# One copy of 1024 columns instead of two of 512, for the last two scores of an attention phase

## The chip, the cores and the metric

The kernel runs on one core of a Trainium2 chip. The core has five engines with queues of their own: TensorE (PE, its loads of weights shown apart as PEld), VectorE (DVE), ScalarE (ACT), GpSimd (POOL) and SyncE (SP, which issues transfers here). Matmuls write to PSUM, which has 8 banks of 512 f32 columns on 128 partitions; ACT and DVE read them from there into SBUF. The metric is the device time of one execution in microseconds. A profile comes from one such execution.

## The reference

Two branches work on the same x (2048 rows of 512) and are mixed row by row:

```python
g = sigmoid((x * gate_w).sum(-1, keepdims=True))
a = softmax_attention(x, wqkv, H=32, Dh=16) @ wo
b = mixer_mlp(x, w1, b1, w2, b2)     # LayerNorm, then an MLP with gelu across the 2048 rows
out = g * a + (1 - g) * b
```

For each of 32 heads the attention takes the scores of all 2048 queries against all 2048 keys (inner size 16), their exp, the product with v, and a division by the row sums. This part holds the change.

## The kernel before, in words

The kernel first makes v, the keys, half of the queries and the first layer of the MLP, up to about 280 us. The attention then runs in `NG * PHASES` = 32 x 4 = 128 phases. A group (`grp`) is a pair of heads and one half of the 1024 + 1024 queries; each of its four phases (`ph`) takes 16 scores. A score is one matmul of 128 keys by 512 queries (f32 results, one bank), line 1067, and each score stands in one half of TensorE's rows. In the other half a dense matmul (line 1076, tile `dn`) runs beside it: the second layer of the MLP, late queries and the output projection are cut into lists of 14 or 12 of these.

The 16 scores of a phase have numbers, and the number says what becomes of them:

- `SINGLE` (0, 2, 4, 6, 7, 8): ACT takes the exp of one bank, line 1093, tile `p`.
- `EVAC` (1, 3, 5, 9, 14, 15): DVE copies the bank into the SBUF tile `pe`, line 1089; when all six are there, ACT takes the exp of the 3072 columns in place, line 1102.
- `TWO` (10, 11) and (12, 13): two neighbouring banks, tile `t`, one exp of 1024 columns by ACT, line 1031.

Then 64 matmuls of `apply_v` (line 963, tile `av`) multiply exps by v: first those held over from the phase before (the `pe` tile), then this phase's single exps and pairs. DVE adds `av` to the group's sum (line 985). The next phase's scores follow at once. So the `pe` tile is used a phase later than it is made.

Seven banks serve the scores (`BANKS = 7`), the eighth the dense matmuls. `shares(n)` gives the order in which a phase takes them. Scores 0 to 6 take `share[0]` to `share[6]`; 7, 8 and 9 take the first three again; 10 and 11 take `share[3]` and `share[4]`, 12 and 13 `share[5]` and `share[6]`; 14 takes `share[0]` and 15 `share[2]`, both under the name `u`; `av` takes `share[1]`, and this bank becomes `share[6]` of the next phase. A matmul that writes a bank waits until the last reader of the bank is done: score 14 for ACT's exp of score 7, score 15 for DVE's copy of score 9, `av` for ACT's exp of score 8. Each `t` pair waits for a copy of DVE and an exp of ACT.

The order of the work on each engine in the attention is that of the code (`manual_schedule`). `later`, `amid` and `calls` put other work between: `amid` stands ahead of the copies of scores 14 and 15 on DVE, `later` behind the exp of the 3072 columns. Where the list of dense matmuls has 12, the last scores come in the order 12, 13, 15, 14.

Of the kernel before, what the change touches and what calls it, by code (L numbers as in the profile page):

```python
# [9 lines left out]
F32 = mybir.dt.float32  # L10
# [13 lines left out]
P = 128  # L24
# [8 lines left out]
NB = 512  # L33
# [27 lines left out]
def gated_mix(ctx: ExitStack, tc: tile.TileContext, a_x, a_wqkv, a_wo, b_w1, b_b1, b_w2, b_b2, gate_w, out):  # L61
    nc = tc.nc
# [115 lines left out]
    with tc.tile_pool(name="vp", bufs=1, side="right") as pool:  # L178
# [143 lines left out]
        y, t, w = (pool.tile([P, NS], F32, name=n) for n in "ytw")  # L322
# [103 lines left out]
    with tc.tile_pool(name="gl", bufs=2, side="right") as gl:  # L426
# [74 lines left out]
        for f0, cs in order.items():  # L501
            n = min(NB, F - f0) // P
# [43 lines left out]
    for i, p in reversed(list(enumerate(ps))):  # L546
        u = out_pool.tile([P, D], F32, name="row", bufs=3)
# [329 lines left out]
    for t in range(NS):  # L877
        at = put(second_layer(t), at, [14] * 3)
        if queries:
            b, n = queries.pop(0)  # L880
# [39 lines left out]
    TWO = (10, 11), (12, 13)  # L920
# [3 lines left out]
    def shares(n):  # L924

        for one in range(0, BANKS, 2):
            lows = [k for k in range(one)][::2] + [k for k in range(one + 1, BANKS)][::2]
            for third in lows:
                if n in (third, third + 1):
                    first, second = (low for low in lows if low != third)  # L930
                    return [first, first + 1, one, second, second + 1, 2 * third + 1 - n, n]


    def regions():
        return tc.tile_pool(name="ps_s", bufs=1, space=PSUM, reuse_waits="tile")
# [54 lines left out]
    with tc.manual_schedule(engines=engines):  # L990
# [3 lines left out]
        for p in range(LAST + 1):  # L994
            grp, ph = divmod(p, PHASES)
            second = ph % 2
# [20 lines left out]
            in_turn = list(range(n_b)) + ([14, 15] if n_b == NSC - 2 else [12, 13, 15, 14])  # L1017
            qbs = {}
            for a, b in TURNS + HELD:
                if head[a] == head[b]:  # L1020
                    qbs[a], qbs[b] = 0, 1
                else:
                    zero, one = (a, b) if head[a] == 0 else (b, a)
# [3 lines left out]
            def exps(n):  # L1027
                pt = ptp.tile([P, 2, NB], F32, name="p2", bufs=len(TWO))
                where = [share[(j - BANKS) % BANKS] for j in (n - 1, n)]
                low = min(where)  # L1030
                pairs_done.append(nc.scalar.activation(pt, twos[low, low + 1], AF.Exp, scale=SCALE))  # L1031
                for j, k in zip((n - 1, n), where):
                    units[j] = *units[j][:3], pt[:, k - low, :]

            pairs_done = []
            evac = evp.tile([P, len(EVAC), NB], F32, name="pe")
            units = {}
            share = shares(spare)
            pool = regions()
            psum = pool.__enter__()  # L1040
            ones = [psum.tile([P, NB], F32, name=f"s{n}") for n in range(BANKS)]
            for n in in_turn:
                i, qb = head[n], qbs[n]
                c = at[i][qb]
                at[i][qb] += 1
                if n < TWO[0][0]:
                    if n >= BANKS:
                        ones[share[n - BANKS]] = psum.tile([P, NB], F32, name=f"s{share[n - BANKS]}")
                    s = ones[share[n % BANKS]]
                else:  # L1050
                    if n == TWO[0][0]:
                        pool.__exit__(None, None, None)
                        pool = regions()
                        psum = pool.__enter__()
                        twos = {}
                        for low in range(BANKS):
                            if low == share[1]:
                                av = psum.tile([P, NB], F32, name="av")
                            elif low in (share[0], share[2]):
                                twos[low] = psum.tile([P, NB], F32, name=f"u{low}")  # L1060
                            elif low not in twos:
                                two = psum.tile([P, 2, NB], F32, name=f"t{low}")
                                twos[low], twos[low + 1] = two[:, 0, :], two[:, 1, :]
                                twos[low, low + 1] = two
                    s = twos[share[2 if n == NSC - 1 else (n - BANKS) % BANKS]]
                rows_i = slice(i * HALF, i * HALF + ROWS)
                nc.tensor.matmul(  # L1067
                    s,
                    kt[grp][rows_i, c * P : (c + 1) * P],
                    qt[grp][rows_i, qb * NB : (qb + 1) * NB],  # L1070
                    start=True,
                    stop=True,
                )
                if n < n_b:
                    ps, a, b, begin, last, done = beside[n]
                    mm = nc.tensor.matmul(ps, a[half], b[half], start=begin and not second, stop=last and bool(second))  # L1076
                    if n == 0 and fence is not None:
                        tc.add_manual_dep(mm.ins, fence.ins.name, SYNC, reason=REASON)
                    if n == n_b - 1:
                        fence = nc.gpsimd.memset(token, 0.0)  # L1080
                        tc.add_manual_dep(fence.ins, mm.ins.name, SYNC, reason=REASON)
                if n == in_turn[-2]:
                    if n_b and second and beside[-1][-1] in between:
                        between[beside[-1][-1]]()
                    for what, *args in amid.get(p, ()):
                        what(*args)
                if n in EVAC:
                    pt = evac[:, EVAC.index(n), :]
                    nc.vector.tensor_copy(pt, s)  # L1089
                    units[n] = i, c, qb, pt  # L1090
                elif n in SINGLE:
                    pt = ptp.tile([P, NB], F32, name="p1", bufs=len(SINGLE))
                    one = nc.scalar.activation(pt, s, AF.Exp, scale=SCALE)  # L1093
                    if n == SINGLE[-1] and p:
                        tc.add_manual_dep(one.ins, earlier.ins.name, SYNC, reason=EARLY)
                    units[n] = i, c, qb, pt
                else:
                    units[n] = i, c, qb, None
                    if n in (TWO[0][1], TWO[1][1]):
                        exps(n)  # L1100
# [129 lines left out]
    with tc.If(far_off != 0):  # L1230
        with (
# [6 lines left out]
            for b in range(ND):  # L1238
                with tc.For_i(0, P // DH, 1) as hi:
# [11 lines left out]
                    for t in range(NS):  # L1251
                        s = ps_s.tile([P, S], F32, name="s")
# [11 lines left out]
                        for n in range(NQ):  # L1264
# [4 lines left out]
                            pt = pool.tile([P, NB // P, P], F32, name="pt")  # L1269
# [41 lines left out]
```

## Time and profile before

| | us |
|---|---|
| median of 3 runs | 1265.4 (1265.24 to 1265.51) |
| the profiled execution | 1265.31 |
| its span, first to last instruction | 1263.5 |
| TensorE's granted clock, mean | 0.999 |
| 128 phases, first to last score | from 277.5 to 1224.6 |

Each row of a timeline has start and length in us, engine, line, operation, result and operands, a count where neighbours are merged, and in brackets the idle time ahead of it and what ended it. Where several instructions stand in one row the length runs from the first start to the last end, and instructions of an engine may overlap. PE's ends are modelled; its loads of weights (PEld) show when a matmul was let go.

### The profile page before, as it was taken

The page shows a single profiled execution, that of the slowest core. Times are in us where ns is not written, and L with a number is a line of the kernel's source. Part 1 is how long each engine was busy: PE and PEld are TensorE (multiplying, and loading weights), DVE is VectorE, ACT ScalarE, POOL GpSimd, SP SyncE. Part 2 cuts the span into 40 slices and gives each one's busy share as a digit, 9 for nine tenths or more (in the row PEclk, how much of TensorE's full clock was granted, in tenths as well). Part 3 has the DMA queues.
Part 4 walks back from the last instruction along what each step waited for, and adds up shares of the span by engine and source line. Part 5 has one row for each costly group of instructions (what it writes and reads, how often), then busy time and mean ns, then how long its engine had stood idle before and what let it go on. Part 6 is the DMA issues. An engine that isn't in the chain of part 4 may idle for free.

```text
span 1263.5 us, 32833 instructions
## 1 busy us (share of the span) xinstructions
PE 1254.8 (99%) x13342; PEld 829.2 (66%) x13342; DVE 856.7 (68%) x1562; ACT 1069.0 (85%) x1405; POOL 198.6 (16%) x316
## 2 busy tenths in 40 slices
PE   9999999999999999999999999999999999999998
PEld 7888888875666666666666666666666666666656
DVE  5675453178767676767677677776777677678883
ACT  4443343269999999999999999999999999999990
POOL 0220444461010101010110101111111111000000
PEclk9999999999999999999999999999999999999999
DMA  4799443244744444544344433444543443366611
GB/s 134 251 340 329 143 122 106 81 127 110 214 121 104 90 102 85 158 86 97 77 105 94 99 90 83 91 87 81 113 101 73 90 100 60 56 166 175 151 60 70
DMA packets 100556, 152.32 MB, mean 121 GB/s; under 512 B 17109, under 2 KB 56171, under 8 KB 96300
## 3 DMA queue, kind: packets, MB, share of 16 engines
q1 hardware_dynamic: 99820, 149.08, 46.0%
q8 instruction: 107, 1.75, 0.6%
q10 hardware_dynamic: 576, 1.05, 0.2%
q14 instruction: 53, 0.43, 0.1%
HBM read 105.39 MB, written 44.68 MB: 119 GB/s over the span
## 4 chain that ended last, share of the span: by engine, by line
PE 96%; DVE 2%; ACT 1%; issue 0%; DVEq 0%
PE av L963 31%; PE s L1067 21%; PE acc L424 12%; PE t L1067 9%; PE acc L75 8%; PE t L963 5%; PE dn L1076 3%; PE u L1067 3%; PE pa L1162 2%; DVE pe L1089 1%; PE acc L199 1%; PE acc L268 0%; DVE ot L985 0%; PE acc L245 0%; ACT p L1093 0%; ACT pe L1102 0%
## 5 line engine op out<-in xcount | busy, mean ns | idle before, releaser
L1093 ACT ACTIVATE p<-s 128x512 f32<-128x512 f32 x768 | 411.9, 789 | 0.1
L1102 ACT ACTIVATE pe<-pe 128x3072 f32<-128x3072 f32 x129 | 380.9, 2954 | 0.0
L1067 PE MATMUL s<-qs,ks 64*128 64x512 f32 x1280 | 329.8, 400 | 0.6 <-ACT p L1093 0.6
L1089 DVE COPY pe<-s 128x512 f32<-128x512 f32 x512 | 323.6, 685 | 5.5 <-PE s L1067 1.5
L1067 PEld LDWEIGHTS s<-qs,ks 64*128 64x128 f32 x1280 | 225.7, 184 | 92.7 <-issue 52.3
L1031 ACT ACTIVATE p<-t 128x1024 f32<-128x1024 f32 x256 | 278.7, 1267 | 0.0
L963 PE MATMUL av<-p,v 128*32 128x256 f32 x3880 | 227.2, 379 | 0.0
L1089 DVE COPY pe<-u 128x512 f32<-128x512 f32 x256 | 164.8, 685 | 67.1 <-PE u L1067 67.1
L963 PE MATMUL av<-pe,v 128*32 128x256 f32 x3072 | 192.5, 383 | 0.0
L985 DVE TENSOR_TENSOR ot<-av,ot 128x512 f32<-128x512 f32 (+2 forms) x160 | 93.0, 582 | 140.9 <-PE av L963 139.6
L68 POOL TENSOR_TENSOR w_lo<-w_raw,w_hi 128x512 fp32r<-128x512 f32 (+1 forms) x128 | 153.0, 1202 | 196.8 <-ACT w_hi L67 99.9
L1076 PE MATMUL dn<-u_lo,w_hi 64*128 64x512 f32 x448 | 181.0, 404 | 0.0
L1076 PE MATMUL dn<-u_hi,w_hi 64*128 64x512 f32 x448 | 180.7, 403 | 0.0
L963 PEld LDWEIGHTS av<-p,v 128*32 128x32 f32 x3880 | 126.0, 110 | 83.3 <-ACT p L1093 0.2
L1076 PE MATMUL dn<-u_hi,w_lo 64*128 64x512 f32 x448 | 180.6, 403 | 0.0
L1067 PE MATMUL t<-qs,ks 64*128 64x512 f32 x512 | 142.5, 413 | 0.0
L963 PEld LDWEIGHTS av<-pe,v 128*32 128x32 f32 x3072 | 86.8, 109 | 80.7 <-ACT p L1093 35.7
L1080 POOL MEMSET token<- 1x1 f32 x128 | 11.3, 88 | 742.7 <-PE dn L1076 679.4
L67 ACT CAST w_hi<-w_raw 128x512 fp32r<-128x512 f32 (+1 forms) x67 | 38.0, 569 | 82.7 <-PE acc L424 63.1
L1067 PEld LDWEIGHTS t<-qs,ks 64*128 64x128 f32 x512 | 73.2, 184 | 50.8 <-ACT p L1093 48.6
L424 PE MATMUL acc<-h_hi,w_hi 128*128 128x512 f32 x224 | 87.9, 392 | 0.0
L424 PE MATMUL acc<-h_hi,w_lo 128*128 128x512 f32 x224 | 87.9, 392 | 0.0
(171 smaller groups left out, 1615.8 us busy)
## 6 DMA issues: line engine op xcount, KB each, us to landing
w_raw<-in_B_w_dram SPq DMA_DIRECT2D x96, 256.0 KB
ks<-kp SPq DMA_DIRECT2D x192, 128.0 KB
qs<-qp SPq DMA_DIRECT2D x256, 64.0 KB
kp<-pc SPq DMA_DIRECT2D x16, 512.0 KB
qp<-pc SPq DMA_DIRECT2D x8, 768.0 KB
qp<-row SPq DMA_DIRECT2D x24, 256.0 KB
v<-v SPq DMA_DIRECT2D x4, 1088.0 KB
x<-in_A_x_dram SPq DMA_DIRECT2D x16, 256.0 KB
```

What stands on the lines that cost most here:

```text
L67: copy(hi, src)
L68: return sub(lo, src, hi.bitcast(F32), ALU.subtract)
L75: nc.tensor.matmul(ps, a, b, start=start and n == 0, stop=stop and n == last)
L424: nc.tensor.matmul(p, a, b, start=first and k == 0, stop=last and k == 2)
L963: mm = nc.tensor.matmul(av[32 * j : 32 * (j + 1), i * QC : (i + 1) * QC], vb[b][:, v_at : v_at + 32], pt[:, h * QC : (h + 1) * QC], start= ...
L985: latest["add"] = nc.vector.tensor_tensor(x, y, x, ALU.add)
L1031: pairs_done.append(nc.scalar.activation(pt, twos[low, low + 1], AF.Exp, scale=SCALE))
L1067: nc.tensor.matmul(s, kt[grp][rows_i, c * P : (c + 1) * P], qt[grp][rows_i, qb * NB : (qb + 1) * NB], start=True, stop=True,)
L1076: mm = nc.tensor.matmul(ps, a[half], b[half], start=begin and not second, stop=last and bool(second))
L1089: nc.vector.tensor_copy(pt, s)
L1093: one = nc.scalar.activation(pt, s, AF.Exp, scale=SCALE)
L1102: done = nc.scalar.activation(x, x, AF.Exp, scale=SCALE)
```

## The change

`shares` now puts the neighbour of the first bank third and the odd bank second, so that scores 14 and 15 stand in neighbouring banks and `av` in the odd one. The two banks become one tile of 1024 columns, still named `u`. The four copies of scores 1, 3, 5 and 9 stay as they are; scores 14 and 15 are copied by one operation, issued behind the later of the two, into the last two slots of `pe`, which are neighbours already.

```diff
-                    return [first, first + 1, one, second, second + 1, 2 * third + 1 - n, n]
+                    return [first, one, first + 1, second, second + 1, 2 * third + 1 - n, n]
...
                             if low == share[1]:
                                 av = psum.tile([P, NB], F32, name="av")
-                            elif low in (share[0], share[2]):
-                                twos[low] = psum.tile([P, NB], F32, name=f"u{low}")
                             elif low not in twos:
-                                two = psum.tile([P, 2, NB], F32, name=f"t{low}")
+                                two = psum.tile([P, 2, NB], F32, name=f"{'u' if low == share[0] else 't'}{low}")
                                 twos[low], twos[low + 1] = two[:, 0, :], two[:, 1, :]
                                 twos[low, low + 1] = two
...
                 if n in EVAC:
                     pt = evac[:, EVAC.index(n), :]
-                    nc.vector.tensor_copy(pt, s)
+                    if n < TWO[0][0]:
+                        nc.vector.tensor_copy(pt, s)
+                    elif n == in_turn[-1]:
+                        nc.vector.tensor_copy(evac[:, -2:, :], twos[share[0], share[2]])
                     units[n] = i, c, qb, pt
```

On TensorE the end of a phase's scores stood like this (names: `t` and `u` the tiles above, `dn` the dense matmul, `av` the product with v; in brackets the semaphores of the engines that the instruction waits for):

```order
L1067 MATMUL t_4040<-qs,ks 128x512 [waits DVE_49,Activation_49]
L1076 MATMUL dn<-u_hi,w_lo 128x512
L1067 MATMUL t_4040<-qs,ks 128x512
L1076 MATMUL dn<-u_hi,w_hi 128x512
L1067 MATMUL u_4038<-qs,ks 128x512 [waits Activation_49]
L1067 MATMUL u_4037<-qs,ks 128x512 [waits DVE_49]
L963 MATMUL av<-pe,v_111 32x256 [waits Activation_49]
```

The same place now:

```order
L1065 MATMUL t_4016<-qs,ks 128x512 [waits DVE_49,Activation_49]
L1074 MATMUL dn<-u_hi,w_lo 128x512
L1065 MATMUL t_4016<-qs,ks 128x512
L1074 MATMUL dn<-u_hi,w_hi 128x512
L1065 MATMUL u_4017<-qs,ks 128x512 [waits DVE_49,Activation_49]
L1065 MATMUL u_4017<-qs,ks 128x512
L963 MATMUL av<-pe,v_111 32x256 [waits Activation_49]
```

The order is the same; the two waits, which stood on one u score each, now stand together on the first. On DVE a phase had, from the sum's addition to the small instruction behind the copies (`mark`):

```order
L985 TENSOR_TENSOR ot<-av,ot 128x512 [waits PE_49]
L1089 COPY pe<-s_3131 128x512 [waits PE_49]
L1089 COPY pe<-s_3132 128x512 [waits PE_49]
L1089 COPY pe<-s_3128 128x512 [waits PE_49]
L1089 COPY pe<-s_3169 128x512 [waits PE_49]
L1089 COPY pe<-u_3179 128x512 [waits PE_49]
L1089 COPY pe<-u_3177 128x512 [waits PE_49]
L1111 MEMSET mark 1x1 [waits DVE_49,Activation_49,Pool_49]
```

And now:

```order
L985 TENSOR_TENSOR ot<-av,ot 128x512 [waits PE_49]
L1088 COPY pe<-s_3121 128x512 [waits PE_49]
L1088 COPY pe<-s_3124 128x512 [waits PE_49]
L1088 COPY pe<-s_3120 128x512 [waits PE_49]
L1088 COPY pe<-s_3161 128x512 [waits PE_49]
L1090 COPY pe<-u_3171 128x1024 [waits PE_49]
L1112 MEMSET mark 1x1 [waits DVE_49,Activation_49,Pool_49]
```

The last two copies are one row; nothing else moved on DVE.

## The prediction

> **What bounds the kernel now.** I read the page first, then a table by stage, then the timeline of single phases on each engine. All rows are of the kernel before.
>
> ```profile
> span 1263.5 us, 32833 instructions
> PE 1254.8 (99%) x13342; PEld 829.2 (66%) x13342; DVE 856.7 (68%) x1562; ACT 1069.0 (85%) x1405; POOL 198.6 (16%) x316
> L1102 ACT ACTIVATE pe<-pe 128x3072 f32<-128x3072 f32 x129 | 380.9, 2954 | 0.0
> L1089 DVE COPY pe<-u 128x512 f32<-128x512 f32 x256 | 164.8, 685 | 67.1 <-PE u L1067 67.1
> ...
> 308.20:1109.40 801.20, 801.12 (x10124) 493.43 (x10120) 572.15 (x1072) 801.20 (x973) 91.63 (x195) 1.00 0.45 100
> 1116.90:1221.20 104.30, 103.74 (x1292) 63.96 (x1288) 88.99 (x160) 104.26 (x127) 3.78 (x18) 1.00 0.59 147
> ```
>
> The last two rows are stretches of the attention phases: length, then busy time of PE, PEld, DVE, ACT and POOL, clock, DMA. PE and ACT are both busy to the last hundredth in the first, so the share of busy time cannot say which of them sets the pace. DVE, from which the change takes work, has 229 us free there (801.2 - 572.2): its time in itself is worth nothing.
>
> What sets the pace is read from one phase, here the one that starts at 805.26.
>
> ```profile
> start us, us, engine line op out<-in xcount [idle before <-releaser]
> 805.26 0.18 PEld L1067 LDWEIGHTS s<-qs,ks 64*128 64x128 f32 x1 [0.41 <-issue]
> 807.72 1.32 ACT L1093 ACTIVATE p<-s 128x512 f32<-128x512 f32 x2
> 807.86 0.69 DVE L1089 COPY pe<-s 128x512 f32<-128x512 f32 x1
> 808.20 0.84 ACT L1093 ACTIVATE p<-s 128x512 f32<-128x512 f32 x1
> 808.60 0.19 PEld L1067 LDWEIGHTS u<-qs,ks 64*128 64x128 f32 x2 [0.19 <-ACT p L1093]
> 809.09 0.16 PEld L963 LDWEIGHTS av<-pe,v 128*32 128x32 f32 x8 [0.30 <-ACT p L1093]
> 809.13 1.29 DVE L1089 COPY pe<-u 128x512 f32<-128x512 f32 x2 [0.58 <-PE u L1067]
> 810.51 3.01 ACT L1102 ACTIVATE pe<-pe 128x3072 f32<-128x3072 f32 x1
> 812.68 0.18 PEld L1067 LDWEIGHTS s<-qs,ks 64*128 64x128 f32 x1 [0.41 <-issue]
> ```
>
> The sixth and last single exp of ACT (score 8) runs from 808.20 to 809.04; its bank is the one that `av` takes, and the first weight load of `av` is at 809.09, 0.05 later. From there 64 `av` matmuls lead to the next phase's first load at 812.68. So ACT's exps hold `av`. The u scores are loaded at 808.60, 0.05 after DVE's fourth copy ended (807.86 + 0.69 = 808.55), and between u load and `av` load lie 0.49 us.
>
> Whether those 0.49 are needed is shown by the last phases, where ACT is not the limit:
>
> ```profile
> 1124.52 0.18 PEld L1067 LDWEIGHTS s<-qs,ks 64*128 64x128 f32 x1 [0.41 <-issue]
> 1126.49 0.68 DVE L1089 COPY pe<-s 128x512 f32<-128x512 f32 x1
> 1126.52 0.61 ACT L1093 ACTIVATE p<-s 128x512 f32<-128x512 f32 x1
> 1127.29 0.18 PEld L1067 LDWEIGHTS t<-qs,ks 64*128 64x128 f32 x1 [0.15 <-ACT p L1093]
> 1127.14 0.69 DVE L1089 COPY pe<-s 128x512 f32<-128x512 f32 x1
> 1127.88 0.19 PEld L1067 LDWEIGHTS u<-qs,ks 64*128 64x128 f32 x2 [0.38 <-DVE pe L1089]
> 1128.32 0.16 PEld L963 LDWEIGHTS av<-pe,v 128*32 128x32 f32 x8 [0.25 <-ACT p L1093]
> 1146.67 0.18 PEld L1067 LDWEIGHTS s<-qs,ks 64*128 64x128 f32 x1 [0.41 <-issue]
> 1154.32 0.18 PEld L1067 LDWEIGHTS s<-qs,ks 64*128 64x128 f32 x1 [0.41 <-issue]
> 1176.43 0.18 PEld L1067 LDWEIGHTS s<-qs,ks 64*128 64x128 f32 x1 [0.41 <-issue]
> ```
>
> Here `av` follows the u load by 1128.32 - 1127.88 = 0.44. So in the long stretch only 0.05 us of slack lies behind the u load. The rows name a second loop, of PE and DVE alone: first score, fourth copy of DVE, u load, `av`, next first score. Its length where nothing else holds it is that of the phases 1124.52 to 1146.67 and 1154.32 to 1176.43, three each: (22.15 + 22.11) / 6 = 7.377 us.
>
> ```profile
> 308.24 0.18 PEld L1067 LDWEIGHTS s<-qs,ks 64*128 64x128 f32 x1 [0.41 <-issue]
> 1116.87 0.18 PEld L1067 LDWEIGHTS s<-qs,ks 64*128 64x128 f32 x1 [0.41 <-issue]
> ```
>
> From 308.24 to 1116.87 there are 109 phases, (1116.87 - 308.24) / 109 = 7.419 each. So ACT's loop is 7.419, the loop of PE and DVE 7.377; the second is covered by 0.042 us a phase.
>
> **The change, part by part.**
>
> *The copy.* Two copies of 512 columns took 1.29 us together (809.13). One of 1024 is not in the trace; its price is bounded by these rows:
>
> ```profile
> L1119 DVE TENSOR_TENSOR e<-o_sum,e 128x1024 fp32r<-128x1024 f32 x2 | 2.4, 1218 | 0.0
> L1119 DVE CAST e<-o_sum 128x1024 fp32r<-128x1024 f32 x2 | 1.4, 691 | 0.0
> L985 DVE TENSOR_TENSOR ot<-av,ot 128x512 f32<-128x512 f32 x95 | 65.6, 690 | 134.4 <-PE av L963 134.1
> L985 DVE TENSOR_TENSOR ot<-av,ot 128x256 f32<-128x256 f32 x34 | 14.2, 421 | 5.5 <-PE av L963 5.5
> ```
>
> At least 0.69 (a cast within SBUF), at most twice 0.685 = 1.37. From PSUM, 256 more columns cost 690 - 421 = 269 ns, so 512 more on a copy of 685 give 685 + 538 = 1.22, as the operation of 1024 columns has; I take 1.22. It saves 0.07 a phase on an engine that isn't on either loop: 0. The fused copy starts only after both scores; PE issues these two together (u x2, one row), so that costs 0 too.
>
> *ACT's exp of 3072 columns* waits for the copies: it starts at 810.51, 0.09 after their end at 810.42. Its start does not set ACT's pace, as one late start shows:
>
> ```profile
> 861.50 1.30 ACT L1031 ACTIVATE p<-t 128x1024 f32<-128x1024 f32 x1
> 862.73 2.77 ACT L1102 ACTIVATE pe<-pe 128x3072 f32<-128x3072 f32 x1
> 864.61 0.18 PEld L1067 LDWEIGHTS s<-qs,ks 64*128 64x128 f32 x1 [0.41 <-issue]
> 872.07 0.18 PEld L1067 LDWEIGHTS s<-qs,ks 64*128 64x128 f32 x1 [0.41 <-issue]
> ```
>
> There it starts 0.07 before its forerunner's end (862.80); in the phase above it started 0.36 before (L1031's pair ran to 810.87). So it is 0.29 late, and the phase behind it lasts 7.46, only 0.04 more than 7.419. ACT holds some 0.25 us of work in hand there, and a start that moves by some hundredths costs or gains 0.
>
> *The banks.* Score 14, 15 and `av` change places among the banks. Every bank but that of `av` is released long before it is written: the last copy ended at 810.42, the next phase's first load is at 812.68. The bank of `av` stays last in the next phase's order, as before. 0.
>
> *The wait of the u scores.* This is the part that costs. Before, score 14 waits for ACT alone and score 15 for DVE alone. As one tile both waits stand on the first of them, as they stood on each `t` pair already. PE then spends an instruction on the second wait:
>
> ```profile
> L1067 PEldq EVENT_SEMAPHORE  x297: 51/51/51, 274.7 to 1223.9; - x149
> ```
>
> 297 of them before, 51 ns each, two a phase for the two `t` pairs; now a third. Its price where DVE is the later releaser is read from the phase at 1124.52: the `t` load with two waits comes at 1127.29, 0.12 after DVE's copy (1127.17; ACT was done at 1127.13), the u load with one wait comes at 1127.88, 0.05 after its copy (1127.83). So 0.07, between 0.05 (the 51 ns alone) and 0.08 (two roundings of 0.01 each way); I take 0.06, between the instruction's own length and the difference. A gain is excluded, since the wait is only added. Behind this wait PE's own queue stands: both u loads, `av`'s 64 matmuls, then the next scores.
>
> **The sum.** In the 109 phases of the long stretch the loop of PE and DVE grows from 7.377 to 7.437 and overtakes ACT's 7.419: 0.018 x 109 = 2.0 us. ACT then runs out of its work in hand and waits, which costs nothing more. In the phases after 1116.87, 15 with the last, DVE releases the u load already (the row at 1127.88 says so): 0.06 x 15 = 0.9. The first four phases wait for other things: 0. Together 2.9 us. The profiled execution took 1265.31 (its span of 1263.5 and 1.8 around it); the median of the three runs, 1265.4, stands 0.1 above. 1265.3 + 2.9 = 1268.2, or 0.23% more. With 0.05 as the price it is 109 x 0.008 + 15 x 0.05 = 1.6, so 1266.9; with 0.08, 109 x 0.038 + 15 x 0.08 = 5.3, so 1270.6.
>
> **The rivals.**
>
> *The wait is hidden.* If PE resolves the wait for DVE ahead, or it is ACT's that goes into the extra instruction, `av` moves by two hundredths at most where ACT is the limit, and not at all in the last phases: ACT's fifth exp (807.72, the first of the two, some 0.83 long) ends with DVE's copy at 808.55, so `av` would come at 808.55 + 0.12 + 0.44 = 809.11 against 809.09. In the long stretch that is between 0 and 109 x 0.02 = 2.2 us, 1265.3 to 1267.5. For it: the covered 0.05 is real. Against it: the `t` loads put DVE's wait in front, in the same order of names as the u load now has. The Trainium skill, VectorE: DVE Perf Modes, § The DRAIN you can't avoid, says of a row of DVE copies that "the semaphore costs nothing extra here". By that rule, carried over to PE, the time would stay at 1265.3; the trace has 0.12 against 0.05 for two waits and one on PE, so I don't carry it over.
>
> *Faster: ACT's long exp starts earlier.* Its place is the start at 810.51. If the u load weren't later, the fused copy would end at 809.13 + 1.22 = 810.35 in place of 810.42. The second exp of 1024 columns could let its follower in at 810.48 (the pair's start 808.67 plus twice 0.91, the spacing of the two: 2.20 - 1.29), so 0.03 earlier in 128 phases: 3.8 us, 1261.5. It decides from the point where ACT's pace hangs on that start. For it: ACT is never idle, and the exp does start 0.09 behind the copy. Against it: the 0.29 that cost 0.04, and the u scores' 0.06, which uses up the 0.07 saved.
>
> *Slower by more: the fused copy ends late.* At 1.37 and 0.06 later it would end at 810.56, 0.14 late; if half of it came through in the 109 phases, that is 7.6 on top of the 2.9, 1275.8. The Trainium skill, Perfetto Trace Analysis, § Optimizing Scalar/DVE Operations, says that where DVE isn't saturated but causes bubbles, breaking up instructions may let work end sooner; that speaks against fusing. The same 0.29 that cost 0.04 says that ACT doesn't feel 0.14.
>
> **How the numbers follow.** The forecast's mechanism has 0.60, the hidden wait 0.28, ACT's earlier exp 0.08, the late copy 0.04. About 0.2%, or 2.5 us, is what a measurement of this kernel can tell from no change; the bound above is 1267.9. The forecast's own bounds, 1266.9 to 1270.6, lie mostly above it: 0.52 of its 0.60 I put to slower and 0.08 to no change. Slower is then 0.52 + 0.04 = 0.56, same 0.28 + 0.08 = 0.36, faster 0.08. The range takes in the hidden wait and the upper bound of the forecast with 0.2 to 0.3 for the spread of runs: 1265.0 to 1270.8. It leaves out the third and fourth case.
>
> **What the profile after would show.** The waiting instructions of the scores' line rise from 297 by 128 to about 425. The u load stands 0.12, not 0.05, behind DVE's fourth copy, and its releaser is DVE in nearly all phases. The phases of the long stretch last 7.43 to 7.44, those of the end 0.06 more each. The fused copy takes 1.22 and ends at the same place in the phase as the two did; ACT's exps show shorter records, since they no longer queue. The forecast is wrong if the phases stay at 7.419 (the wait is hidden), if the u load moves and `av` does not follow it by 0.44, or if the exp of 3072 columns comes to hold the next phase's first score.

## The result, and the profile after

The changed kernel takes 1271.31 us in the median of 5 runs (1271.18 to 1272.25), against 1265.44 (1265.24 to 1265.51) for the kernel before on the same chip: 1.0046 times as long, with a 95% interval of 1.0033 to 1.0058. The prediction was 1268.2, in a range up to 1270.8. The profiled execution took 1271.31, with a span of 1269.5 (before 1263.5), at the same granted clock of 0.999. An execution now and then has a lower granted clock and is longer, as is one of those given below, 1280.94 us at 0.948.

The page of the kernel after: busy time of the engines, the chain that ended last, and three of its costliest groups.

```profile
PE 1256.6 (99%) x13342; PEld 844.4 (67%) x13342; DVE 849.0 (67%) x1434; ACT 1073.9 (85%) x1405; POOL 198.9 (16%) x316
PE 91%; DVE 7%; issue 1%; DMA 0%; ACT 0%; SPq 0%; DVEq 0%; ACTq 0%
L1094 ACT ACTIVATE p<-s 128x512 f32<-128x512 f32 x768 | 390.9, 622 | 0.0
L1103 ACT ACTIVATE pe<-pe 128x3072 f32<-128x3072 f32 x129 | 356.4, 2764 | 1.1 <-DVE pe L1090 0.9
L1090 DVE COPY pe<-u 128x1024 f32<-128x1024 f32 x128 | 156.7, 1225 | 79.7 <-PE u L1065 79.1
```

The fused copy takes 1.225 us, and DVE is less busy by 7.7 us (856.7 to 849.0). Yet the span is 6.0 us longer. ACT's records of 3072 columns fell from a mean of 2954 to 2764 ns, though the operation is the same: part of the longer record was waiting in ACT's own queue (rows of ACT that show it stand with the rivals below).

The first loads of the phases that begin and end the long stretch, and the stretches as the kernel after has them (columns as in the prediction):

```profile
308.36 0.18 PEld L1065 LDWEIGHTS s<-qs,ks 64*128 64x128 f32 x1 [0.41 <-issue]
1121.49 0.18 PEld L1065 LDWEIGHTS s<-qs,ks 64*128 64x128 f32 x1 [0.41 <-issue]
308.36:1121.49 813.13, 810.65 (x10216) 512.98 (x10212) 570.37 (x973) 812.93 (x982) 91.79 (x195) 1.00 0.45 100
1121.49:1227.01 105.52, 103.68 (x1293) 64.29 (x1289) 88.37 (x146) 104.87 (x127) 3.79 (x18) 1.00 0.56 143
```

The same 109 phases took 813.13 us instead of 808.63, or 7.460 each instead of 7.419: +4.5 us. The next 14 took 105.52. Before, by the trace's nanoseconds, these 14 took 104.37, so +1.14. The first four phases add 0.15, and the last phase and what follows it 0.23: 0.15 + 4.49 + 1.14 + 0.23 = 6.0. The share of busy time still says nothing of who sets the pace: ACT shows 812.93 of 813.13, though, as the next rows show, it is ahead of its work now.

The waiting instructions of the scores' line, in the list of that line's instructions (count, shortest, median and longest in ns):

```profile
L1065 PEldq EVENT_SEMAPHORE  x424: 51/51/51, 274.7 to 1230.3; - x142
```

There were 297, so 127 were added. And the end of one phase, the one that starts at 808.13:

```profile
808.13 0.18 PEld L1065 LDWEIGHTS s<-qs,ks 64*128 64x128 f32 x1 [0.41 <-DVE big L68]
808.66 3.05 ACT L1094 ACTIVATE p<-s 128x512 f32<-128x512 f32 x6
808.89 2.53 DVE L1088 COPY pe<-s 128x512 f32<-128x512 f32 x4
811.53 0.22 PEld L1065 LDWEIGHTS u<-qs,ks 64*128 64x128 f32 x2 [0.31 <-ACT p L1094]
811.99 1.02 PEld L963 LDWEIGHTS av<-pe,v 128*32 128x32 f32 x24 [0.24 <-ACT p L1094]
812.10 1.22 DVE L1090 COPY pe<-u 128x1024 f32<-128x1024 f32 x1 [0.68 <-PE u L1065]
813.41 2.77 ACT L1103 ACTIVATE pe<-pe 128x3072 f32<-128x3072 f32 x1
815.58 0.18 PEld L1065 LDWEIGHTS s<-qs,ks 64*128 64x128 f32 x1 [0.41 <-issue]
```

Three things are to be seen. ACT's six single exps end at 808.66 + 3.05 = 811.71, and `av` is loaded 0.28 later, at 811.99; before, it was 0.05 later. ACT no longer holds `av`. DVE's fourth copy ends at 808.89 + 2.53 = 811.42 and the u load comes at 811.53, 0.11 to 0.12 behind. (The bracket names ACT, whose exp of score 7 was done long before; the wait is for DVE.) And the row of the two u loads is 0.22 long, not 0.19: one load takes 0.183, so the second begins 0.033 behind the first, where it had been 0.003.

In the trace's nanoseconds a phase's loop, from first score to next first score, is made of these parts. "Late, before" is the mean of the six phases from which the prediction took 7.377:

| part of the loop, us | late, before | long stretch, after (mean of 109) |
|---|---|---|
| first score to the end of DVE's fourth copy | 3.297 | 3.295 |
| to the first u load | 0.053 | 0.116 |
| to the second u load | 0.003 | 0.033 |
| to the first `av` load | 0.430 | 0.423 |
| to the next phase's first score | 3.593 | 3.593 |
| sum | 7.376 | 7.460 |

The added wait costs 0.063 at the first load and 0.030 more at the second, less 0.007 at `av` and 0.002 at the copy, 0.084 in all.

### The profile page after: what moved, and what is told of

Same layout as the page of the kernel before. It is cut to its first block, busy times and chain, and to the rows that moved or that the text cites. A ratio compares the mean times of both kernels' runs of the same rounds, so it can differ in the third digit from the quotient of the medians.

```text
span 1269.5 us, 32832 instructions
## 1 busy us (share of the span) xinstructions
PE 1256.6 (99%) x13342; PEld 844.4 (67%) x13342; DVE 849.0 (67%) x1434; ACT 1073.9 (85%) x1405; POOL 198.9 (16%) x316
## 4 chain that ended last, share of the span: by engine, by line
PE 91%; DVE 7%; issue 1%; DMA 0%; ACT 0%; SPq 0%; DVEq 0%; ACTq 0%
PE av L963 30%; PE s L1065 18%; PE acc L424 12%; PE acc L75 8%; PE t L1065 7%; PE t L963 5%; DVE pe L1088 5%; PE u L1065 4%; PE dn L1074 3%; PE pa L1163 2%; DVE ot L985 1%; PE acc L199 1%; PE acc L268 0%; DMA x<-in_A_x_dram 0%; DVE e L1120 0%
## 5 line engine op out<-in xcount | busy, mean ns | idle before, releaser
L1094 ACT ACTIVATE p<-s 128x512 f32<-128x512 f32 x768 | 390.9, 622 | 0.0
L1103 ACT ACTIVATE pe<-pe 128x3072 f32<-128x3072 f32 x129 | 356.4, 2764 | 1.1 <-DVE pe L1090 0.9
L1031 ACT ACTIVATE p<-t 128x1024 f32<-128x1024 f32 x256 | 256.7, 1095 | 0.0
L1090 DVE COPY pe<-u 128x1024 f32<-128x1024 f32 x128 | 156.7, 1225 | 79.7 <-PE u L1065 79.1
L1065 PE MATMUL t<-qs,ks 64*128 64x512 f32 x512 | 135.3, 398 | 0.0
L1065 PEld LDWEIGHTS t<-qs,ks 64*128 64x128 f32 x512 | 81.4, 184 | 32.4 <-ACT p L1094 22.6
```

Source lines behind the costliest of these rows:

```text
L1065: nc.tensor.matmul(s, kt[grp][rows_i, c * P : (c + 1) * P], qt[grp][rows_i, qb * NB : (qb + 1) * NB], start=True, stop=True,)
L1090: nc.vector.tensor_copy(evac[:, -2:, :], twos[share[0], share[2]])
L1103: done = nc.scalar.activation(x, x, AF.Exp, scale=SCALE)
```

## The experiments

The theory is that the added waiting instruction on the first u score makes the whole loss. Its rivals are that the new banks, or the fused copy that can begin only when both scores are there, have a part in it. The first four kernels tell these apart; the last two ask why the price is 0.084 a phase and not 0.06.

**Banks alone.** The kernel before, with nothing but the new order of banks; scores 14 and 15 stay two tiles, with two copies.

```diff
-                    return [first, first + 1, one, second, second + 1, 2 * third + 1 - n, n]
+                    return [first, one, first + 1, second, second + 1, 2 * third + 1 - n, n]
```

> The kernel before with the new order of the banks alone: scores 14 and 15 in neighbouring banks, av in the odd one, but two tiles u with a wait each, and two copies. Theory (the two waits on one load cost the time): the time of before, 1265.4 within 0.5, and phases of 7.419 us in the long stretch. Rival, the banks: all of the loss, 1271.3. Rival, the fused copy: the time of before.

Measured: 1265.32 us (1264.92 to 1266.4, 11 runs), a ratio of 1.0 (0.9991 to 1.0009). The banks cost nothing. The list of the score line's instructions has the old count:

```profile
L1067 PEldq EVENT_SEMAPHORE  x297: 51/51/51, 274.4 to 1223.4; - x149
```

**One tile, two copies.** The kernel after, but with the two banks copied out by two operations of 512 columns, issued together behind the last score.

```diff
                     elif n == in_turn[-1]:
-                        nc.vector.tensor_copy(evac[:, -2:, :], twos[share[0], share[2]])
+                        for m, where in enumerate((share[0], share[2])):
+                            nc.vector.tensor_copy(evac[:, len(EVAC) - 2 + m, :], twos[where])
```

> The changed kernel with the one tile u, so with both waits on its first load, but copied out by two copies of 512 issued together. Theory: the time of the changed kernel, 1271.3 within 0.7, since the first u load still stands 0.116 us behind DVE's fourth copy and the second 0.033 behind the first. Rival, the fused copy delays ACT's exp of 3072 columns: back to 1265.4. Rival, the banks: 1271.3.

Measured: 1271.6 (1271.42 to 1271.98), ratio 1.0049 (1.0035 to 1.0062), phases of the long stretch 7.459. The loss stands without the fused copy. The phase that starts at 808.13 here too:

```profile
811.52 0.21 PEld L1065 LDWEIGHTS u<-qs,ks 64*128 64x128 f32 x2 [0.30 <-ACT p L1095]
812.10 1.29 DVE L1091 COPY pe<-u 128x512 f32<-128x512 f32 x2 [0.69 <-PE u L1065]
813.48 2.77 ACT L1104 ACTIVATE pe<-pe 128x3072 f32<-128x3072 f32 x1
815.58 0.18 PEld L1065 LDWEIGHTS s<-qs,ks 64*128 64x128 f32 x1 [0.41 <-issue]
```

The two copies take 1.29 where the one took 1.22, and ACT's long exp starts 0.07 later (813.48, not 813.41). The next phase starts at 815.58 in both: what the fused copy saves is worth 0 here.

**The wait alone.** The kernel before, with its banks, two tiles and two copies, and both waits set on the first issued u score.

```diff
+                if n == in_turn[-2]:
+                    for other in (7, 9):
+                        tc.add_manual_dep(score.ins, done_with[other].ins.name, SYNC, reason=EARLY)
```

(`done_with` holds the copy or exp that read each score.)

> The kernel before, old banks and two copies, with nothing but both waits put on the first u score that is issued (for ACT's exp of score 7 and DVE's copy of score 9); the second u score then waits for nothing of its own. Theory: the whole loss, 1271.3 within 0.7, phases of 7.45 to 7.46 us. Rivals, banks or fused copy: 1265.4.

Measured: 1271.14 (1271.02 to 1271.5), ratio 1.0045 (1.0031 to 1.0059). The long stretch has 7.460 a phase, as after. The list of the line's instructions, and the u and `av` loads of the phase that starts at 808.11:

```profile
L1067 PEldq EVENT_SEMAPHORE  x424: 51/51/51, 274.7 to 1230.3; - x142
...
811.52 0.21 PEld L1067 LDWEIGHTS u<-qs,ks 64*128 64x128 f32 x2 [0.31 <-ACT p L1097]
811.97 1.02 PEld L963 LDWEIGHTS av<-pe,v 128*32 128x32 f32 x24 [0.24 <-ACT p L1097]
```

The wait alone gives the whole loss. Of the changed kernel's three parts (banks, one copy, one wait), this is the one that counts.

**The wait moved.** The kernel after, with the wait for ACT's exp of score 7 set on score 13, ahead of the u scores; the first u score then has DVE's wait only.

```diff
+                if n == TWO[1][1]:
+                    tc.add_manual_dep(score.ins, done_with[7].ins.name, SYNC, reason=EARLY)
```

> The changed kernel with the wait for ACT's exp of score 7 put on score 13, two matmuls ahead, which waits for nothing else; the first u load then waits for DVE alone. Theory: the u load stands 0.053 us behind DVE's copy again and the second 0.003 behind it, and the time is that of before or up to 1.2 us above it (1265.4 to 1266.6), since score 13 now waits for ACT and ACT has less work in hand. Rivals, banks or fused copy: 1271.3.

Measured: 1266.28 (1265.96 to 1280.94, 11 runs), ratio 1.0018 (0.9997 to 1.004): not to be told from no change, and 5 us below the kernel after. The phases have 7.4205 on the mean. The list, and loads, copies and ACT's last single exp of the phase whose u load is at 1128.53:

```profile
L1065 PEldq EVENT_SEMAPHORE  x296: 51/51/51, 274.9 to 1224.9; - x148
...
1127.79 0.69 DVE L1090 COPY pe<-s 128x512 f32<-128x512 f32 x1
1128.09 0.65 ACT L1096 ACTIVATE p<-s 128x512 f32<-128x512 f32 x1
1128.30 0.18 PEld L1065 LDWEIGHTS t<-qs,ks 64*128 64x128 f32 x1 [0.18 <-ACT p L1096]
1128.53 0.19 PEld L1065 LDWEIGHTS u<-qs,ks 64*128 64x128 f32 x2
1128.96 1.02 PEld L963 LDWEIGHTS av<-pe,v 128*32 128x32 f32 x24 [0.25 <-ACT p L1096]
1129.08 1.22 DVE L1092 COPY pe<-u 128x1024 f32<-128x1024 f32 x1 [0.60 <-PE u L1065]
```

The copy ends at 1128.48 and the u load comes 0.05 behind; the pair is 0.19 long again. So the first load's delay and the second's lag go with the waiting instruction. This kernel has the new banks and the fused copy without the added waiting instruction, and with them it is not faster than before. ACT's loop sets the pace again, but by another way than before. ACT's last single exp ends at 1128.74, 0.22 ahead of `av` (0.05 before), so it doesn't hold `av`. Its exp of score 7 holds score 13, whose load (1128.30) comes 0.05 behind that exp on the mean, and `av` follows this load by 0.66. In the trace's nanoseconds ACT's first single exp of a phase ends 0.487 us behind its long exp's end, as before; in the kernel after it was 0.521, because ACT had to wait.

**The second load alone.** This asks whether the 0.030 at the second load matters. The kernel before, with an instruction of GpSimd at the start of the phase, done long before it is needed; the second issued u score waits for it, and for its own releaser.

```diff
+            on_pool = nc.gpsimd.memset(early, 0.0)
...
+                if n == in_turn[-1]:
+                    tc.add_manual_dep(score.ins, on_pool.ins.name, SYNC, reason=EARLY)
```

> The kernel before with a small GpSimd instruction at each phase's start, long done when it is asked for, whose wait is put on the second u score that is issued. Where that is score 15, it then has two waits (DVE's copy of score 9, and this one), and the first u score keeps its single wait for ACT. This prices a wait instruction that delays one load only. Theory (a load with two waits stands 0.116 us behind DVE's copy, and it was the further 0.033 by which the second load followed the first that made up the rest of the loss): the second load at 0.116 behind the copy, av 0.421 behind it, so that ACT's loop of 7.419 is just reached: 0.5 to 1.2 us above before, 1265.9 to 1266.6. Rival (any wait instruction ahead of the last u load costs the whole): 1271.

Measured: 1267.8 (1267.31 to 1268.23, 11 runs) against 1265.76, ratio 1.0016 (1.0007 to 1.0025): more than expected. The long stretch took 809.80, +1.2; the late phases 105.29, +0.9 (0.92). It splits by the order of the scores. In 92 phases of the long stretch score 14 is issued first; its load is early, and the second load, DVE's, comes 0.116 behind the copy. `av` follows that second load by 0.43, and the phases have 7.427. Where 15 comes first (17 phases of the long stretch, and all the late ones), the second load waits only for things long done: ACT's exp, 0.2 us before, and GpSimd's instruction. Here are two of the late phases:

```profile
1121.54 0.26 PEld L1068 LDWEIGHTS u<-qs,ks 64*128 64x128 f32 x2 [0.32 <-DVE pe L1092]
1122.03 1.02 PEld L963 LDWEIGHTS av<-pe,v 128*32 128x32 f32 x24 [0.24 <-issue]
1128.96 0.26 PEld L1068 LDWEIGHTS u<-qs,ks 64*128 64x128 f32 x2 [0.35 <-DVE pe L1092]
1129.46 1.02 PEld L963 LDWEIGHTS av<-pe,v 128*32 128x32 f32 x24 [0.24 <-ACT p L1096]
```

The pair is 0.26 long: the second load lies 0.072 behind the first, although its semaphores had been set. In the trace's nanoseconds the waiting instruction begins within 0.01 us of the first load, not earlier, and its 51 ns then stand on the path. The late phases grew by 0.066 each (0.92 / 14), and the 17 have 7.440, where the loop of PE and DVE was 7.377. Of the whole growth the 92 phases make 0.8 us, the 17 make 0.4 and the late ones 0.9; the expectation had nothing for the last two. So `av` follows the second u load, not the first, and a delay of the second load alone lengthens the phase.

**A third semaphore.** To double the cause: the kernel of "the wait alone", with GpSimd's early instruction as a third releaser of the first u score.

```diff
-                    for other in (7, 9):
-                        tc.add_manual_dep(score.ins, done_with[other].ins.name, SYNC, reason=EARLY)
+                    for other in (done_with[7], done_with[9], on_pool):
+                        tc.add_manual_dep(score.ins, other.ins.name, SYNC, reason=EARLY)
```

> The kernel before with three waits on the first u score that is issued: ACT's exp of score 7, DVE's copy of score 9, and a small GpSimd instruction that is long done. The cause is doubled: two wait instructions stand ahead of the load in place of one. Theory (each wait instruction behind the late one takes its 0.051 us and up to 0.025 to go on): the first u load 0.167 to 0.195 behind DVE's copy, the phases 0.05 to 0.08 longer than with one, so 124 times that on top of 1271.2: 1277 to 1281. Rival (the price is that of waiting for DVE ahead of the load, once): 1271.2.

Measured: 1271.46 (1270.99 to 1272.3), ratio 1.0045 (1.0031 to 1.0059), as with two. The miss is explained by the list of instructions:

```profile
L1068 PEldq EVENT_SEMAPHORE  x424: 51/51/202, 274.6 to 1230.1; - x142
```

The count is that of two waits. In the trace one waiting instruction takes the waits for DVE and ACT together, and the load itself the one for GpSimd. The third releaser added no instruction, so the cause was not doubled, and this run says nothing of how the time would grow with a second one. It does show that a releaser that is long done and adds no waiting instruction costs nothing.

## Why the prediction was wrong in its size

*What bounds the kernel* held. ACT's loop of 7.419 and the loop of PE and DVE of 7.377 behind it were read rightly: a delay on the second loop came through after the first 0.042 of it, and ACT then ran ahead (0.28 us from its last single exp to `av`).

*The copy, the banks, ACT's long exp*, each put at 0, were each 0. The fused copy took 1.225 for the forecast 1.22; the kernel with the new banks alone took 1265.32; with two copies in place of one nothing came back. The fused copy ends 0.03 us later in its phase (5.19 against 5.16 us from the first score, in the median), not at the same place as forecast. Two copies that end later still, at 5.26, gave the same phases of 7.46, so this costs nothing here.

*The wait* is the step whose mechanism was right and whose size was wrong. The forecast was one more waiting instruction a phase (about 425; there are 424), the u load at 0.12 behind DVE's copy (0.116), DVE as the last releaser, phases of 7.43 to 7.44 and 0.06 more for each late one. The count and the place came out. The phases are 7.460, and the late ones grew by 0.081 (1.14 / 14). The term that was mis-sized is "I take 0.06". It was the delay of the first u load, 0.063 by the trace, and it left out that the second u load also moves behind the first. Since `av` follows the second load, as the kernel with the second load delayed shows, the price was 0.084. The sum by it: 7.460 - 7.419 = 0.041 a phase, 4.5 us in the 109 phases instead of 2.0, because the cover of 0.042 is taken off once and all of the rest comes through. The late phases, the last with them, gave 1.4 (1.14 + 0.23) instead of 0.9, and the first four 0.15 instead of 0. The bound of 0.08 was too low by 0.004, for the same reason: it was two roundings around the first load.

The kernel before showed the missing term. These are rows of its weight loads alone, in the phase that the prediction used:

```profile
1127.29 0.22 PEld L1067 LDWEIGHTS t<-qs,ks 64*128 64x128 f32 x2 [0.15 <-ACT p L1093]
1127.88 0.19 PEld L1067 LDWEIGHTS u<-qs,ks 64*128 64x128 f32 x2 [0.38 <-DVE pe L1089]
```

The `t` pair behind two waits is 0.22 long and the u pair behind one 0.19. The prediction's row of this `t` load came from a window that ended at 1127.3, ahead of the second load's start, so it counted one load and the 0.03 could not be seen. With 0.06 + 0.03 the same sum would have been 109 x 0.048 + 15 x 0.09 = 6.6, so 1271.9.

*The rivals.* The hidden wait is refuted by the u load at 0.116, whose 51 ns stand behind DVE's copy; in the trace the waiting instruction takes DVE's semaphore in all 128 phases, and the load itself ACT's. The Trainium skill, Perfetto Trace Analysis, § Identifying Dependency Chains, says that an instruction which waits on several engines may get EventSemaphore instructions put ahead of it; the trace agrees (297 to 424). The late fused copy did not occur.

The gain by ACT's earlier exp needs more than the kernel with the wait moved. That one stays at 1266.28, not 1261.5, but its fused copy ends no earlier (5.17 against 5.16 us from the first score), so the rival's condition isn't met there. What decides is ACT's pair and the long exp behind it, first before, then with the wait moved:

```profile
808.67 2.20 ACT L1031 ACTIVATE p<-t 128x1024 f32<-128x1024 f32 x2
810.51 3.01 ACT L1102 ACTIVATE pe<-pe 128x3072 f32<-128x3072 f32 x1
...
1128.57 2.00 ACT L1031 ACTIVATE p<-t 128x1024 f32<-128x1024 f32 x2
1130.39 2.83 ACT L1106 ACTIVATE pe<-pe 128x3072 f32<-128x3072 f32 x1
```

The long exp starts 0.36 ahead of the pair's end in the first and 0.18 ahead in the second, and ends 2.65 behind it in both (810.87 to 813.52, and 1130.57 to 1133.22). The means of the long stretch say the same: 0.35 and 0.17 ahead, 2.65 behind in both. So the earlier start brought no earlier end: ACT's pace doesn't hang on it here.

What remains open is small. In 22 of the 109 phases of the kernel after the fourth copy ends at more than 3.30 us, mostly at 3.33 instead of 3.29, and these phases have 7.49 for the others' 7.45. The kernel before has such phases too (30 of them), where ACT's loop hides them. The copy is not longer there (0.69 in both) but starts 0.04 later; why was not tried. Nor was it tried whether the loss goes away when the waiting instruction takes ACT's semaphore and the load DVE's.

## What to carry to other kernels

Two buffers made into one also put their two releasers on one instruction. Here that was one more waiting instruction on TensorE's queue, and what it costs is decided by where the last releaser stands on the path, not by what the merged operation saves. When such a wait is priced, follow the delay to the load on which the next step really hangs, and read the second instruction behind the wait as well as the first. A loop that is covered by little (here 0.042 us of 7.4) pays every further hundredth in every round.

## What the runs showed of the hardware

- A load behind a waiting instruction on TensorE's queue came 0.116 us behind its releaser instead of 0.053, and the load after it 0.033 behind that instead of 0.003.
- A waiting instruction whose semaphore had long been set still cost: directly behind a load that was itself held, it put the next load 0.072 behind that one, and the late phases grew by 0.066.
- A third releaser on a score that had two added no waiting instruction (424 in both; one took two waits, the load the third) and no time to be told (1271.46 and 1271.14).
- One record of ACT is longer when ACT is the limit: the exp of 512 columns had a mean of 622 ns after, and in the long stretch before, in the view by line, 808; ACT shows as fully busy in both. The exp of 3072 columns ended 2.65 us behind its forerunner whether its record started 0.35 or 0.17 us ahead of the forerunner's end.
